# A searched order of some 2,100 steps replaced by another, v's rows regrouped by pairs of heads, and fewer small scale steps

## The chip, the cores and the metric

The kernel runs on one core of one Trainium2 chip. The metric is the device time of one execution in microseconds (us), and lower is better. The core's engines each work through a list of instructions of their own: TensorE (PE in the profile, and PEld for its weight loads), VectorE (DVE), ScalarE (ACT) and GpSimd (POOL). SyncE (SP) issues the DMA transfers, in order, from one queue.

## The reference

Pooled attention is followed by a small feed-forward layer. What is computed is:

```python
# q, k, v: 8 batches, 8 heads, 576 rows, 64 columns
k_p = k.reshape(B, H, 72, 8, D).mean(axis=3)      # v_p likewise
scores = scale * q @ k_p.T                        # 576 x 72 per head
attn = exp(scores - rowmax) / (rowsum + 1e-9)
x = (attn @ v_p).transpose(0, 2, 1, 3).reshape(4608, 512)
h = x @ w_in                                      # 512 x 1024
e = exp(h - rowmax(h)); sm = e / (sum(e) + 1e-9)
solu = h * sm
ln = (solu - mean) / sqrt(var + 1e-6) * g_ln
out = ln @ w_out                                  # 1024 x 512
```

The weights `w_in` and `w_out` arrive as 8-byte floats and are turned into pairs of 16-bit values on the chip. So are q, k, v and the tensors between the stages: each operand of a product has a high and a low half, and a product is three matmuls (high by high, high by low, low by high).

## The kernel before, in words

The 4608 rows of x are 36 tiles of 128 rows. Nine tiles cover two batches: four of the first, one that mixes the last 64 rows of both, four of the second. Each tile passes through these stages.

1. `q_hi` and `q_lo` split q, and a DMA transpose (`q_T`) turns it. For tile 0 TensorE turns it (`q_Tp`), and ScalarE copies it out (`q_Tc`).
2. `scores` (tile `sc`, 32 matmuls) writes the one score buffer in PSUM. `s_max`, `s_sub`, `s_exp`, `e_sum`, two `e_rec` and `e_mul` are the softmax on VectorE, with the exponential on ScalarE. Only after `e_mul` may the next tile's `scores` write the buffer.
3. `e_hi` (two instructions on ScalarE) and `e_lo` (two on GpSimd) split the result, and `e_T` turns it by DMA (tile 0 again by TensorE, `e_Tp` and `e_Tc`).
4. `av` (tile `xp`, 24 matmuls) multiplies by v. `x_hi` on ScalarE and `x_lo` on VectorE split the result into `xT`.
5. `mm1` (tile `hp`, 48 matmuls of 512 columns in three parts of 16) multiplies by `w_in`. The softmax-weighted activation and the statistics follow (`h_max`, `h_exp`, `z_mul` and others), and two DMA transposes turn the result.
6. `mm2` (tile `op`, 48 matmuls) multiplies by `w_out`, `o_evac` scales by the row's norm, and `o_store` writes out.

Per batch, k and v are pooled over eight rows. GpSimd does it in three levels of adds (`pool_kv`) for three pieces of each (two of 256 rows in 128 partitions, one of 64 rows). For batch 0 TensorE does it (`pool_pe`, tiles `krps` and `vrps`) and ScalarE copies it out (`pool_ev`). A power of two that bounds the pooled tensor is then found: `a_max` reduces along the row (tile `amx`), `a_par` spreads it to all partitions by a small matmul (`gk`, `gv`), `a_all` reduces again (`pk`, `pv`), and three small steps `a_scale` on VectorE make the scale and its inverse (`sk`, `sv`). `v_hi`, `v_x`, `v_lo`, `r_hi`, `r_lo`, `v_rep` and `r_put` then fill the operand `vb` of `av`.

The weights are prepared once, four pieces each. `w_exp` (`u`) and `w_sgn` run on ScalarE, `w_shift`, `w_tail` on VectorE, `w_mul` on GpSimd. `w_bnd` on TensorE finds a bound, from which `wi_scale` and `wo_scale` make the scales. `w_hi` on ScalarE writes the high half. `w_res` (tile `res`, fp32 matmuls on TensorE) and `w_lo` on ScalarE write the low half, or `w_lod` on VectorE alone for the last two pieces of `w_out`.

Nothing schedules this at run time. Each call has a number in the table `ORDER`, the calls are issued in the order of these numbers, and each engine runs its own instructions in that order. A waiting instruction therefore holds back all that stand behind it on its engine, and on SyncE all transfers behind it.

v's 576 pooled rows lie in `vr` as follows. A chunk holds two heads: 64 partitions take the first 64 pooled rows of one head, the other 64 those of the next. The last eight rows of all eight heads are a fifth chunk of 64 partitions. Each piece of two chunks is loaded by two transfers of 64 partitions.

Of the kernel before, what the change touches and what calls it, by code (L numbers as in the profile page):

```python
# [10 lines left out]
F32 = mybir.dt.float32  # L11
# [1535 lines left out]
```

## Time and profile before

| what | value |
|---|---|
| median of three runs | 493.6 us (492.75 to 493.71) |
| profiled execution, its own time | 493.96 us |
| its span, first to last instruction | 492.2 us |
| share of the span in which PE was busy | 94% |
| DVE, ACT, POOL busy | 76%, 67%, 62% |
| first `mm1` of tile 0 starts | 65.35 us |
| last matmul ends | 4.34 us before the span's end |

The span is what the trace covers. The profiled execution's own time is 1.76 us longer, and it lies 0.36 us above the median of the runs. Up to 65 us the weights are prepared, batch 0 is pooled and the pipeline is filled. From there on TensorE works through the tiles.

### The profile page before, as it was taken

The page shows a single profiled execution, that of the slowest core. Times are in us where ns is not written, and L with a number is a line of the kernel's source. Part 1 is how long each engine was busy: PE and PEld are TensorE (multiplying, and loading weights), DVE is VectorE, ACT ScalarE, POOL GpSimd, SP SyncE. Part 2 cuts the span into 40 slices and gives each one's busy share as a digit, 9 for nine tenths or more (in the row PEclk, how much of TensorE's full clock was granted, in tenths as well). Part 3 has the DMA queues.
Part 4 walks back from the last instruction along what each step waited for, and adds up shares of the span by engine and source line. Part 5 has one row for each costly group of instructions (what it writes and reads, how often), then busy time and mean ns, then how long its engine had stood idle before and what let it go on. Part 6 is the DMA issues. An engine that isn't in the chain of part 4 may idle for free.

```text
span 492.2 us, 14712 instructions
## 1 busy us (share of the span) xinstructions
PE 464.2 (94%) x5976; PEld 301.0 (61%) x5976; DVE 371.7 (76%) x808; ACT 332.2 (67%) x521; POOL 305.8 (62%) x520
## 2 busy tenths in 40 slices
PE   3698699999999999999999999999999999999996
PEld 3574355565667667766755555555566666666663
DVE  3898899997888878897859887788778769553320
ACT  4577997857867687767549656766766767674551
POOL 1556654896668686956792687554986437618340
PEclk9999899999999999999999999999999999999999
DMA  8998668997999996997979979998999485647252
GB/s 301 359 309 197 160 103 188 182 215 165 216 213 216 201 217 128 247 178 209 189 174 166 179 200 204 188 143 174 212 215 171 114 156 125 116 102 136 55 117 87
DMA packets 197940, 88.92 MB, mean 181 GB/s; under 512 B 174312, under 2 KB 182512, under 8 KB 197360
## 3 DMA queue, kind: packets, MB, share of 16 engines
q1 hardware_dynamic: 197872, 87.98, 85.8%
q8 instruction: 47, 0.77, 0.7%
q14 instruction: 21, 0.17, 0.1%
HBM read 36.70 MB, written 9.44 MB: 94 GB/s over the span
## 4 chain that ended last, share of the span: by engine, by line
PE 63%; DVE 10%; POOL 10%; DMA 7%; ACT 4%; issue 3%; SPq 2%; POOLq 0%; ACTq 0%; DVEq 0%
PE op L272 27%; PE hp L272 26%; PE xp L998 4%; PE sc L272 3%; POOL vr L395 2%; DMA wir<-in_moe_w_in_dram 2%; DMA zT<-z 2%; DMA vr<-in_v_dram 2%; POOL kr L395 2%; POOL z L1092 2%; PE vrps L405 1%; DVE z L1072 1%; DVE m L1040 1%; POOL kp L395 1%; PE res_wo L809 1%
## 5 line engine op out<-in xcount | busy, mean ns | idle before, releaser
L272 PE MATMUL hp<-wi,xT 128*64 128x512 f16 x1728 | 197.7, 379 | 1.0 <-ACT xT L1007 0.9
L272 PE MATMUL op<-wo,zT 128*64 128x512 f16 x1728 | 197.7, 379 | 0.8 <-DMA zT<-z 0.6
L272 PEld LDWEIGHTS <-xT 128*64 128x64 f16 x1728 | 110.2, 110 | 70.4 <-ACT xT L1007 1.4
L272 PEld LDWEIGHTS <-zT 128*64 128x64 f16 x1728 | 111.3, 110 | 67.0 <-DMA zT<-z 1.1
L1092 POOL TENSOR_TENSOR z<-z,z 128x512 f16<-128x512 f32 x71 | 82.8, 1175 | 56.9 <-ACT z L1086 55.5
L1040 DVE TENSOR_REDUCE m<-hp 128x1 f32<-128x1024 f32 x36 | 43.9, 1218 | 27.1 <-PE hp L272 25.1
L977 POOL TENSOR_TENSOR e<-e,e 128x512 f16<-128x512 f32 x36 | 42.6, 1184 | 31.4 <-ACT e L969 31.3
L1051 ACT ACTIVATE z<-hp,nb,Hb 128x1024 f32<-128x1024 f32 x32 | 38.3, 1198 | 20.3 <-DVE nb L1043 18.4
L1072 DVE SCALAR_TENSOR_TENSOR z<-hp,rs,z 128x1024 f32<-128x1024 f32 x36 | 46.1, 1279 | 5.9 <-ACT z L1051 4.8
L1081 ACT ACTIVATE z<-z,sz 128x1024 f32<-128x1024 f32 x36 | 41.1, 1143 | 13.3 <-DVE z L1072 13.3
L1150 ACT ACTIVATE osb<-op,f 128x512 f32<-128x512 f32 x36 | 24.5, 680 | 29.5 <-PE op L272 23.9
L395 POOL TENSOR_TENSOR kr<-kr 128x512 f32<-128x512 f32 (+3 forms) x42 | 36.9, 886 | 9.3 <-DMA kr<-in_k_dram 8.6
L395 POOL TENSOR_TENSOR vr<-vr 128x512 f32<-128x512 f32 (+3 forms) x42 | 36.7, 878 | 5.7 <-DMA vr<-in_v_dram 3.7
L1086 ACT ACTIVATE z<-z 128x1024 f16<-128x1024 f32 x36 | 37.9, 1052 | 2.0 <-issue 1.4
L933 DVE TENSOR_REDUCE sc<-sc 128x8 f32<-128x576 f32 x36 | 27.4, 761 | 14.9 <-ACT sc L929 14.9
L1105 ACT ACTIVATE junk<-z 128x1024 f16<-128x1024 f32 x36 | 37.7, 1048 | 0.2
L919 DVE TENSOR_REDUCE mx<-sc 128x8 f32<-128x576 f32 x36 | 27.0, 750 | 10.7 <-PE sc L272 10.7
L998 PEld LDWEIGHTS <-vb 128*64 128x64 f16 x960 | 29.1, 111 | 7.0 <-DMA eT<-e 1.3
L998 PE MATMUL xp<-eT,vb 128*64 128x128 f16 (+1 forms) x960 | 31.1, 215 | 1.2 <-DMA eT<-e 0.9
L272 PEld LDWEIGHTS <-qT 128*64 128x64 f16 x1152 | 25.0, 114 | 9.0 <-issue 5.1
L272 PE MATMUL sc<-kT,qT 128*64 128x72 f16 x1152 | 25.9, 200 | 3.8 <-DVE e L948 2.7
L1011 DVE SCALAR_TENSOR_TENSOR xT<-xp,xT 128x512 f16<-128x512 f32 x36 | 24.6, 683 | 5.7 <-ACT xT L1007 5.5
(239 smaller groups left out, 625.8 us busy)
## 6 DMA issues: line engine op xcount, KB each, us to landing
kr<-in_k_dram SPq DMA_DIRECT2D x16, 512.0 KB, 5.3
qr<-in_q_dram SPq DMA_DIRECT2D x16, 512.0 KB, 5.8
vr<-in_v_dram SPq DMA_DIRECT2D x32, 256.0 KB, 5.4
out_dram<-osb SPq DMA_DIRECT2D x32, 256.0 KB, 4.3
wor<-in_moe_w_out_dram SPq DMA_DIRECT2D x4, 1024.0 KB
wo<-in_moe_w_in_dram SPq DMA_DIRECT2D x2, 1024.0 KB
wir<-in_moe_w_in_dram SPq DMA_DIRECT2D x2, 1024.0 KB, 10.9
zT<-z SPq DMA_TRANSPOSE x72, 3.9
```

The lines of the kernel that those rows point to most:

```text
L272: nc.tensor.matmul(out[lo : lo + 64] if m > 64 else out, lhsT=lhsT[:, lo : lo + 64], **kw)
L395: nc.gpsimd.tensor_tensor(out=dst, in0=src[:, :, :n], in1=src[:, :, n : 2 * n], op=ALU.add)
L933: nc.vector.tensor_reduce(out=tl[i]["r0"], in_=s_view(i), axis=AX.X, op=ALU.add)
L977: nc.gpsimd.tensor_tensor(out=e_main(i, 1), in0=e_src(i)[0], in1=e_main(i, 0), op=ALU.subtract)
L998: nc.tensor.matmul(xp[64 * e : 64 * e + 64, c, lo:hi], lhsT=vb[b % 2][:, n, c, e], rhs=eT[:, 2 * c + e if n < 2 else H + c // 2, lo:hi], s ...
L1040: nc.vector.tensor_reduce(out=small(i, "m"), in_=tl[i]["hp"], axis=AX.XY, op=ALU.max)
L1051: nc.scalar.activation(z, t["hp"], AF.Exp, bias=t["nb"], scale=hsc(i, 0), accum_out=small(i, "se"))
L1072: nc.vector.scalar_tensor_tensor(out=t["z"], in0=t["hp"], scalar=t["rs"], in1=t["z"], op0=ALU.mult, op1=ALU.mult, accum_out=small(i, "sz"),)
L1081: nc.scalar.activation(t["zf"], t["zf"], AF.Identity, bias=t["sz"], scale=-float(DFF))
L1086: nc.scalar.activation(t["z16"][:, 0], t["zf"], AF.Copy)
L1092: eng.tensor_tensor(out=t["z16"][:, 1, fs], in0=t["zf"][:, fs], in1=t["z16"][:, 0, fs], op=ALU.subtract)
L1105: nc.scalar.activation(junk, t["zf"], AF.Square, scale=DFF**-0.5, accum_out=small(i, "V"))
```

## The change

Four things change.

- v: the 144 pooled rows of a pair of heads are taken as one run. Rows 8 to 135 are the pair's chunk of 128 partitions. Rows 0 to 7 and 136 to 143 go to the fifth chunk, in partitions 0 to 31 for the first head of each of the four pairs and 32 to 63 for the second. A piece of two chunks is one transfer of 128 partitions, the fifth chunk two of 32. `sel`, `e_src`, `e_rest` and the last operand of `av` follow the new places, and the second step of `e_hi` becomes two instructions.
- Small steps: `identb` carries the factor 2^-14, and `exp_bits` sets the lowest exponent itself. `a_scale` with three steps becomes `a_unit` with two. `wi_scale` and `wo_scale` lose steps, and two small products (`w_pwi`, `w_pwo`) go to GpSimd.
- `g_all` takes on the bound of `g_ln`, which stood in `wo_scale`.
- `ORDER` is new throughout. In it the three loads of batch 0's k stand otherwise among those of the weights, and v's among those of `w_out`.

```diff
 ORDER = {
-        "a_all.k": (37, 200, 454, 660, 903, 1143, 1391, 1620),
+        "a_all.k": (36, 188, 449, 652, 881, 1126, 1380, 1614),
...
-            out=dst.bitcast(I32), in0=src.bitcast(I32), scalar1=EXPMASK, scalar2=None,
-            op0=ALU.bitwise_and,
+            out=dst.bitcast(I32), in0=src.bitcast(I32), scalar1=EXPMASK, scalar2=1 << 23,
+            op0=ALU.bitwise_and, op1=ALU.bitwise_or,
...
-    nc.vector.tensor_copy(out=identb, in_=ident)
+    nc.vector.tensor_scalar(out=identb, in0=ident, scalar1=1.0 / S14, scalar2=None, op0=ALU.mult)
...
-        rows = v[b].rearrange("h (r j) d -> h r (j d)", j=POOL)
+        rows = v[b].rearrange("h (r j) d -> (h r) (j d)", j=POOL).rearrange(
+            "(c r) x -> r c x", c=CI
+        )
         if part < 2:
+            eng.dma_start(t[:, c0:c1], rows[POOL : POOL + P, c0:c1])
+        else:
             for e in range(2):
-                eng.dma_start(
-                    t[64 * e : 64 * e + 64, c0:c1],
-                    rows[2 * c0 + e : 2 * c1 : 2, :64].rearrange("c r x -> r c x"),
-                )
-        else:
-            eng.dma_start(t[:64, CI], rows[:, 64:])
+                r0 = e * (POOL + P)
+                eng.dma_start(t[32 * e : 32 * e + 32, CI], rows[r0 : r0 + POOL])
...
-    def a_scale(nm, key, n):
+    def a_unit(nm, key, n):
         st = grp[nm, key]
         if n == 0:
-            nc.vector.tensor_scalar(
-                out=st["p"], in0=st["p"], scalar1=1e-30, scalar2=1.0 / S14, op0=ALU.max,
-                op1=ALU.mult,
-            )
-        elif n == 1:
             exp_bits(st["p"], st["p"])
         else:
             nc.vector.reciprocal(out=st["s"], in_=st["p"])
...
     def wi_scale():
-        w_bound("wi")
-        nc.vector.tensor_scalar(
-            out=pwi, in0=wst["wi"]["gm"], scalar1=1.0 / S14, scalar2=None, op0=ALU.mult
-        )
+        w_bound("wi", 1.0 / S14)
         sw = const.tile([P, 1], F32, name="sw_wi")
-        nc.vector.reciprocal(out=sw, in_=pwi)
+        nc.vector.reciprocal(out=sw, in_=wst["wi"]["gm"])
         wst["wi"]["s"] = sw
-        for n, c in enumerate((2.0**-11, -(2.0**-11), 2.0**-7)):
-            nc.vector.tensor_scalar(
-                out=pw3[:, n : n + 1], in0=pwi, scalar1=c, scalar2=None, op0=ALU.mult
-            )
-
+
+    def w_pwi():
+        nc.gpsimd.tensor_scalar(
+            out=pw3, in0=c3, scalar1=wst["wi"]["gm"], scalar2=None, op0=ALU.mult
+        )
...
         else:
-            nc.scalar.activation(
-                e_rest(i)[:, ::2],
-                e_src(i)[1].unsqueeze(1).to_broadcast([P, 2, 2, HB, POOL]), AF.Copy
-            )
+            for t in (0, 2):
+                nc.scalar.activation(e_rest(i)[:, t], e_src(i)[1], AF.Copy)
...
-                            rhs=eT[:, 2 * c + e if n < 2 else H + c // 2, lo:hi],
+                            rhs=eT[:, 2 * c + e if n < 2 else H + e, lo:hi],
```

Three places of the new order follow. The first is VectorE where batch 0's v has been pooled. `amx_v`, `gv`, `pv` and `sv` are the steps of v's scale, the rows with `sc`, `mx` and `r` are the softmax of tile 1, and `q_3` and `q_2` are the low halves of q. Before:

```order
L425 TENSOR_REDUCE amx_v<-vp_89 128x1
L919 TENSOR_REDUCE mx_491<-sc_458 128x8
L487 TENSOR_REDUCE pv_502<-gv_499 128x1
L922 TENSOR_TENSOR sc_458<-sc_458,mx_491 128x2x288
L865 SCALAR_TENSOR_TENSOR q_3_507<-qr_204,sq('b', 0)_210,q_3_507 128x8x64
L686 TENSOR_REDUCE g_wo<-bnd_wo 128x1
L865 SCALAR_TENSOR_TENSOR q_2_386<-qr_204,sq('b', 0)_210,q_2_386 128x8x64
L492 TENSOR_SCALAR pv_502<-pv_502 128x1
L933 TENSOR_REDUCE sc_458<-sc_458 128x2x4
L275 TENSOR_SCALAR pv_502<-pv_502 128x1
L939 TENSOR_SCALAR sc_458<-sc_458 128x2x4
L499 RECIPROCAL sv_503<-pv_502 128x1
```

And now:

```order
L430 TENSOR_REDUCE amx_v<-vp_89 128x1
L492 TENSOR_REDUCE pv_520<-gv_517 128x1
L277 TENSOR_SCALAR pv_520<-pv_520 128x1
L499 RECIPROCAL sv_521<-pv_520 128x1
L686 TENSOR_REDUCE g_wo<-bnd_wo 128x1
```

Between the first and the last step of v's scale stood seven rows of other work and one step that the change drops. None of the eight is there now. One of the two `q` rows stands earlier, the other later.

The second place is TensorE ahead of the first `hp`, from the last fp32 product of `res_wo` that stands before `av` of tile 0. `sc` is here the scores of tile 3. Lines of three points leave out the repeats of a row. Before:

```order
L272 MATMUL sc_747<-kT_296,qT_660 64x72
...
L809 MATMUL res_wo_783<-wor_272,dg_wo_696 128x512
L812 MATMUL res_wo_783<-wo,minus 128x512
...
L998 MATMUL xp_790<-eT_723,vb_91 64x128
...
L272 MATMUL hp_819<-wi,xT_815 64x512
```

And now:

```order
L810 MATMUL res_wo_718<-wor_288,dg_wo_641 128x512
L813 MATMUL res_wo_718<-wo,minus 128x512
...
L999 MATMUL xp_727<-eT_659,vb_91 64x128
...
L274 MATMUL sc_765<-kT_300,qT_714 64x72
...
L274 MATMUL hp_803<-wi,xT_800 64x512
```

The scores of tile 3 moved from ahead of `res_wo` to between `xp` and `hp`.

The third place is the start of SyncE's queue: `wo` and `wir` are the pieces of `w_in`, `wor` those of `w_out`, `kr`, `qr` and `vr` batch 0's k, q and v. Before:

```order
L351 DMA kr_140<-in_k_dram 128x2x512
L623 DMA wo<-in_moe_w_in_dram 128x2048 x2
L355 DMA kr_140<-in_k_dram 64x512
L623 DMA wir_184<-in_moe_w_in_dram 128x2048
L351 DMA kr_140<-in_k_dram 128x2x512
L371 DMA qr_204<-in_q_dram 128x4x256 x2
L623 DMA wir_255<-in_moe_w_in_dram 128x2048
```

And now:

```order
L623 DMA wo<-in_moe_w_in_dram 128x2048 x2
L360 DMA kr_158<-in_k_dram 64x512
L623 DMA wir_169<-in_moe_w_in_dram 128x2048
L356 DMA kr_158<-in_k_dram 128x2x512 x2
L376 DMA qr_182<-in_q_dram 128x4x256 x2
L623 DMA wir_222<-in_moe_w_in_dram 128x2048
```

The first large piece of k moved from the head of the queue to behind the third piece of `w_in`, beside the second.

## Rows read from the trace of the kernel before

**Rows 1.** The page: busy time, share of the span and instructions by engine.

```profile
PE 464.2 (94%) x5976; PEld 301.0 (61%) x5976; DVE 371.7 (76%) x808; ACT 332.2 (67%) x521; POOL 305.8 (62%) x520
```

**Rows 2.** Windows: busy us of PE, PEld, DVE, ACT, POOL, then PEclk, DMA, GB/s.

```profile
40.34:65.35 25.01, 18.88 (x201) 9.01 (x200) 22.30 (x54) 20.57 (x36) 19.17 (x26) 0.93 0.69 168
65.35:487.86 422.51, 418.60 (x5554) 269.65 (x5554) 320.63 (x690) 285.91 (x456) 272.14 (x478) 1.00 0.87 171
487.86:492.20 4.34, 0.00 (x0) 0.00 (x0) 0.00 (x0) 0.69 (x1) 0.00 (x0) 0.92 0.17 62
```

**Rows 3.** Timeline of PE: start, duration, what, idle before and its releaser.

```profile
15.13 3.79 PE L405 MATMUL krps<-kr,ident 128*128 128x128 f32 x16 [1.14 <-DMA kr<-in_k_dram]
...
37.73 0.44 PE L272 MATMUL g_g<-ident,g_g 128*64 128x128 f32 x4
38.10 0.37 PE L650 MATMUL bnd_wo<-pmat,u_wo 128*128 128x32 bf16 x8
38.31 2.03 PE L405 MATMUL vrps<-vr,ident 128*128 128x128 f32 x16
...
41.50 0.25 PE L272 MATMUL gv<-identb,amx_v 128*64 128x128 bf16 x2 [0.52 <-DVE amx_v L425]
...
45.55 0.44 PE L272 MATMUL g_wo<-ident,g_wo 128*64 128x128 f32 x4 [0.98 <-DVE g_wo L686]
...
49.99 0.38 PE L812 MATMUL res_wi<-wi,minus 128*128 128x512 f16 x1 [0.68 <-ACT wi L788]
...
52.49 0.71 PE L272 MATMUL sc<-kT,qT 128*64 128x72 f16 x32 [1.01 <-DVE e L948]
53.94 1.46 PE L809 MATMUL res_wo<-wor,dg_wo 128*128 128x512 f32 x2 [0.73 <-POOL vr L395]
...
60.73 0.71 PE L272 MATMUL sc<-kT,qT 128*64 128x72 f16 x32 [1.53 <-DVE e L948]
...
65.35 3.64 PE L272 MATMUL hp<-wi,xT 128*64 128x512 f16 x32 [0.69 <-ACT xT L1007]
```

**Rows 4.** Timeline of PE near the end.

```profile
466.94 20.91 PE L272 MATMUL op<-wo,zT 128*64 128x512 f16 x192
```

**Rows 5.** Timeline of DVE from the pooling of batch 0's v.

```profile
40.95 0.49 DVE L425 TENSOR_REDUCE amx_v<-vp 128x1 bf16<-128x320 f32 x1 [2.28 <-ACT vp L416]
...
42.88 2.28 DVE L865 SCALAR_TENSOR_TENSOR q<-qr,sq('b', 0)_210,q 128x512 f16<-128x512 f32 x1
...
45.42 1.81 DVE L865 SCALAR_TENSOR_TENSOR q<-qr,sq('b', 0)_210,q 128x512 f16<-128x512 f32 x1
...
48.09 0.15 DVE L499 RECIPROCAL sv<-pv 128x1 f32<-128x1 f32 x1
```

**Rows 6.** Timelines of POOL and ACT in the same stretch.

```profile
42.10 2.51 POOL L395 TENSOR_TENSOR kr<-kr 64x256 f32<-64x256 f32 x3
45.41 1.28 POOL L395 TENSOR_TENSOR vr<-vr 128x512 f32<-128x512 f32 x1 [0.80 <-DMA vr<-in_v_dram]
...
48.34 0.51 ACT L568 ACTIVATE vb<-vp,sv 64x256 f16<-64x256 f32 x1 [2.67 <-DVE sv L499]
```

**Rows 7.** Groups on DVE and ACT by line: busy, mean ns of one.

```profile
L865 DVE SCALAR_TENSOR_TENSOR q<-qr,sq('b', 7)_7329,q 128x512 f16<-128x512 f32 x4 | 2.9, 736 | 1.7 <-ACT q L861 1.7
L492 DVE TENSOR_SCALAR pv<-pv 128x1 f32<-128x1 f32 x8 | 1.2, 150 | 0.1
L971 ACT ACTIVATE e<-e 128x128 f16<-128x128 f32 x36 | 10.8, 299 | 7.4 <-DVE e L948 5.4 <-POOL f L1126 1.0 <-DMA eT<-e 1.0
```

**Rows 8.** Windows: TensorE's clock between 54 and 58 us; DVE up to 120 us.

```profile
54.00:56.00 2.00, 2.00 (x4) 0.97 (x5) 1.93 (x6) 1.47 (x4) 1.12 (x2) 0.64 1.05 218
56.00:58.00 2.00, 2.00 (x5) 0.26 (x3) 1.36 (x4) 1.50 (x3) 1.26 (x1) 0.50 0.76 220
65.35:120.00 54.65, 52.98 (x764) 32.59 (x766) 51.38 (x112) 42.74 (x68) 37.85 (x62) 1.00 0.95 181
```

**Rows 9.** The tile vr: issue of v's transfers, ns min/median/max.

```profile
L360 SPq DMA_DIRECT2D vr<-in_v_dram x32: 596/615/2004, 13.2 to 355.7; - x32
```

More of the change, by code (lines that the diff above doesn't have):

```diff
@@ new lines @@
+        1852, 1920, 1939, 1997, 1972),
+        "e_T": (221, 239, 275, 332, 402, 425, 572, 497, 628, 712, 641, 761, 825, 873, 933, 957,
+        1078, 1145, 1146, 1248, 1263, 1356, 1406, 1476, 1495, 1557, 1647, 1634, 1718, 1748, 1851,
+        1887, 1908, 1996, 1942),
+        "e_Tc": (181,),
+        "e_Tp": (180,),
+        "e_hi": (107, 108, 218, 219, 237, 222, 273, 272, 329, 330, 399, 373, 423, 422, 509, 508,
[4 rows of a table added]
+        "e_lo": (109, 220, 238, 274, 331, 401, 424, 571, 496, 604, 711, 640, 760, 824, 861, 932,
@@ new lines @@
+        926, 1023, 1106, 1049, 1200, 1238, 1274, 1345, 1425, 1379, 1502, 1581, 1564, 1655, 1704,
+        1784, 1824, 1864, 1954, 1917),
+        "g_T": (93,),
+        "g_all": (122,),
+        "g_max": (96,),
+        "g_par": (121,),
+        "g_put": (94,),
+        "h_bat": (245, 283, 679, 904, 1060, 1182, 1535, 1839),
+        "h_exp": (265, 325, 362, 441, 457, 545, 614, 623, 697, 751, 857, 828, 936, 954, 1005,
+        1037, 1151, 1185, 1258, 1300, 1384, 1402, 1486, 1510, 1612, 1618, 1679, 1796, 1720, 1832,
@@ new lines @@
+        1823),
+        "v_rep": (192, 318, 542, 833, 1101, 1243, 1498, 1847),
+        "v_x": (214, 196, 296, 328, 586, 607, 879, 849, 1166, 1172, 1286, 1247, 1625, 1540, 1828,
+        1821),
+        "w_all.wi": (66,),
+        "w_all.wo": (143,),
+        "w_bnd.wi": (47, 48, 49, 52),
+        "w_bnd.wo": (73, 126, 127, 136),
+        "w_dg.wi": (68,),
+        "w_dg.wo": (175, 145),
+        "w_exp.wi": (1, 8, 13, 41),
+        "w_exp.wo": (55, 78, 88, 104),
+        "w_hi.wi": (117, 90, 74, 106),
@@ new lines @@
+        "w_hi.wo": (151, 149, 240, 310),
+        "w_lo.wi": (150, 132, 89, 172),
+        "w_lo.wo": (249, 174),
+        "w_load": (0, 6, 12, 40, 54, 77, 86, 103),
+        "w_lod.wo": (344, 324, 321, 316),
+        "w_mul.wi": (5, 19, 17, 64),
+        "w_mul.wo": (61, 84, 156, 251),
+        "w_par.wi": (65,),
+        "w_par.wo": (138,),
+        "w_pwi": (69,),
+        "w_pwo": (353,),
+        "w_res.wi": (148, 125, 75, 171),
+        "w_res.wo": (210, 173),
+        "w_rmax.wi": (53,),
@@ new lines @@
+        "w_rmax.wo": (137,),
+        "w_sgn.wi": (2, 7, 15, 63),
+        "w_sgn.wo": (60, 83, 111, 246),
+        "w_shift.wi": (3, 9, 14, 42),
+        "w_shift.wo": (56, 81, 98, 105),
+        "w_tail.wi": (4, 18, 16, 51),
+        "w_tail.wo": (58, 82, 110, 250),
+        "wi_scale": (67,),
+        "wo_scale": (144,),
+        "x_hi": (226, 258, 277, 334, 384, 464, 507, 589, 563, 662, 782, 723, 843, 895, 953, 981,
+        1013, 1112, 1191, 1207, 1288, 1330, 1399, 1434, 1513, 1547, 1629, 1702, 1658, 1757, 1788,
@@ L325 @@
     nc.gpsimd.memset(phalf, -0.5)
+    for n, c in enumerate((2.0**-11, -(2.0**-11), 2.0**-7)):
+        nc.gpsimd.memset(c3[:, n : n + 1], c)
     for t in vp:
@@ L1211, in scale @@
                 w=[("p" + nm, key), ("s" + nm, key)])
-        for j in range(3):
-            n_ = op("dve", 0.16, t + 0.7 + 0.2 * j, a_scale, nm, key, j, u=[("p" + nm, key)],
+        for j in range(2):
+            n_ = op("dve", 0.16, t + 0.7 + 0.2 * j, a_unit, nm, key, j, u=[("p" + nm, key)],
                     w=[("s" + nm, key)], after=[n_])
@@ L1319, in weight @@
         if nm == "wi":
-            op("dve", 0.9, t_sum + 0.8, wi_scale, r=[("g2", nm)], w=[("ws", nm)])
+            op("dve", 0.5, t_sum + 0.8, wi_scale, r=[("g2", nm)], w=[("ws", nm)])
+            op("pool", 0.3, t_sum + 1.5, w_pwi, r=[("ws", nm)], w=[("pw3",)])
         else:
@@ L1326, in weight @@
             op("dve", 0.28, t_sum - 2, g_all, r=[("x", "gg")], w=[("gg2",)])
-            op("dve", 1.2, t_sum + 0.8, wo_scale, r=[("g2", nm), ("gg2",)], w=[("ws", nm)])
+            op("dve", 0.5, t_sum + 0.8, wo_scale, r=[("g2", nm), ("gg2",)], w=[("ws", nm)])
+            op("pool", 0.3, t_sum + 1.5, w_pwo, r=[("ws", nm)], w=[("pwo",)])
         if nm == "wi" and any((nm, c) not in LO_DVE for c in range(4)):
```

311 lines of the change are left out of this document (134 added, 177 removed), and 90 rows, old and new, of the table ORDER.

## The prediction

> **What bounds the kernel now.** I read the page first. TensorE is busy 94% of the span, and no other engine is above 76% [rows 1]. So TensorE is the first suspect, and what counts is where it stood idle. The windows answer that [rows 2]. I cut the span at three points: the end of the last pooling product of batch 0's v (38.31 + 2.03 = 40.34 us), the first `mm1` (65.35 us) and the end of the last `mm2` [rows 3, 4]. From 65.35 us on TensorE is busy 418.60 of 422.51 us, so 3.91 us are idle there. Behind the last matmul come 4.34 us of evacuation and store. In the 25.01 us before the first `mm1` TensorE is busy 18.88 and idle 6.13. The end of the kernel is therefore the start of the first `mm1`, plus a fixed amount of matmul work, plus 3.91 us of idle time, plus 4.34.
>
> The 6.13 us are told one by one by the timeline of PE [rows 3]: 0.52 (`gv` waits for `amx_v`), 0.98 (`g_wo`), 0.68 (`res_wi` waits for ScalarE's `w_hi`), 1.01 and 1.53 (`scores` of tiles 2 and 3 wait until `e_mul` has freed the score buffer), 0.73 (`res_wo`) and 0.69 (`mm1` waits for `x_hi`). They sum to 6.14.
>
> Behind these waits stands VectorE. `amx_v` runs at 40.95, but v's inverse scale is ready only after 48.09 + 0.15 [rows 5]. Two low halves of q stand in between, and they take 2.28 and 1.81 us [rows 5] where the undisturbed form takes 0.74 [rows 7]. During both GpSimd pools k and v [rows 6]. They lose 1.54 + 1.07 = 2.6 us. ScalarE waits 2.67 us for that scale, with `w_hi` behind [rows 6].
>
> **What stays the same.** The count of matmuls of every kind is unchanged. In both orders three `scores`, three `res_wi`, two `res_wo`, one `av` and the small products lie between the last pooling product and the first `mm1`, and the last four tiles of `mm2` close the program as one block of 192 matmuls [rows 4]. I cost the tail at 0.
>
> **Term A, the start of the first `mm1`.** I go through the idle times with the new order.
>
> - `scores` of tile 3 stands behind `av` now. Its 0.71 us of work cover the wait for `x_hi`, and it no longer waits for `e_mul`: 1.53 + 0.69 = 2.2 us less.
> - `gv` stands behind one `res_wi` (two pairs of rows, over 2 us of work) instead of next to `scores`: 0.5 less.
> - The `w_hi` that was late behind ScalarE's wait for v's scale stands ahead of that wait: 0.7 less.
> - `g_wo`, `scores` of tile 2 and `res_wo` keep their 0.98 + 1.01 + 0.73, since the steps that they wait for are still the last ready.
> - One group of bound products and `g_g` move from ahead of 40.34 to behind it: 0.37 + 0.44 = 0.8 more [rows 3].
> - The first `res_wi` now stands ahead of all v pooling and waits for `wi_scale`, while k's pooling starts later. A large piece of k takes TensorE 3.79 us early in the program [rows 3], and both large pieces now arrive back to back. The bounds are 0 (transfers hide it) and 3.8 (one whole piece late). The total of bytes ahead of the last piece of `w_in` is unchanged, and one of the two pieces can start before the other lands, so I take 0.8, near the lower end.
> - The granted clock is 0.64 and 0.50 from 54 to 58 us, after a stretch of idle waits [rows 8]. [...] With fewer waits ahead this may not happen. Bounds: 0 and 1.7 less. I take 0.8 less.
>
> Sum: -2.2 - 0.5 - 0.7 + 0.8 + 0.8 - 0.8 = -2.6 us. The first `mm1` starts at about 62.7.
>
> **Term B, idle time behind it.** It can fall by 3.9 at most. It can grow, because VectorE is busy 51.38 of 54.65 us up to 120 us [rows 8]: a pipeline that starts 2.6 us earlier needs 2.6 us less VectorE time. There are two sources. Up to the eighth `h_max`, eleven small steps fewer stand in VectorE's list (three each of k's and v's scales, four of `wi_scale`, two of `wo_scale`, and one product more). At 0.15 each [rows 7] that is 1.65 us. The two stalls of the low halves are another 2.6, if they don't come back. 4.25 is more than 2.6, so the idle time should not grow. I take a quarter off: -1.0. Bounds: -3.9 and +2.6.
>
> **Costed at nothing.** The second step of `e_hi` is two instructions for one of 0.30 [rows 7], at most 0.3 us more per tile on ScalarE. ScalarE has 136.6 us idle of 422.51 [rows 2], so this hides behind the matmuls of tiles ahead. Without that cover it would be 36 x 0.3 = 10.8 us. The large pieces of v need one issue for two of 0.62 [rows 9], and the small one two for one, so SyncE issues four transfers per batch instead of five, while TensorE works on earlier tiles. One product per weight on GpSimd (`w_pwi`, `w_pwo`) is first needed by `h_bat` and `n_f`, behind `mm1`.
>
> **Sum.** The profiled execution took 493.96, 1.76 of it outside the span. 493.96 - 2.6 - 1.0 = 490.4. The median of the runs lay 0.4 below the profiled one, so I predict 490.0. The measurement can tell about 0.2% (1 us) from no change, so "faster" is below 492.6.
>
> **Rivals.**
>
> *More.* The order takes nearly all waits away: A = -5.3 (the kept 2.7 go too), and B = -2.6, two thirds of the idle time. That gives 493.6 - 7.9 = 485.7. For it: none of the waits is a transfer from memory. Against: VectorE's 94% busy stretch. Chance 0.17.
>
> *Given back.* The start is earlier by 2.6, but VectorE is no further at 120 us, because its relief doesn't come true, and B grows by 2.6: 493.6. For it speaks the same 94%. Chance 0.13.
>
> *Stalls move.* The order only shifts the collisions: GpSimd keeps its adds, and other steps of VectorE last longer instead. Then VectorE's relief is the small steps alone, and A keeps only the move of `scores` with the extra work, -2.2 + 0.8 = -1.4: 492.2. The low half of q shows what a collision costs: it ended 0.55 us after the three adds of 2.51 us that began at 42.10 [rows 5, 6], so it waited for more than one of them. [...] Chance 0.10.
>
> *Slower.* k is late. If the second large piece of k starts only when the first is through, and both at the slow rate of 3.79, then k's scale, its transpose, the four bounds of `w_in` behind them on TensorE, `wi_scale` and the first `res_wi` all move by 3.8, and the waits behind keep their length because ScalarE's list (weights, exponentials, v) is late with them. The one saving that is left is that of `scores`, against 0.8 of moved work: 493.6 + 3.8 + 0.8 - 2.2 = 496.0. It decides where the last pooling product of v ends more than 2.6 us after 40.34. For it: both pieces behind the third piece of `w_in`. Against: the first has its data earlier. Chance 0.13.
>
> **How the numbers follow.** The forecast has 0.47, with a range of its own of 488.0 to 492.2. With "more" (0.17) and "stalls move" (0.10) it makes most of "faster": 0.72. "Same" is most of "given back" and the upper edge of "stalls move": 0.13. "Slower" is k's delay and the rest: 0.15. The range reaches from "more" to just past "given back": 485.5 to 494.5. It leaves out k's delay and a little below.
>
> **What would show it.** In the changed kernel the first `mm1` starts between 61 and 64 us. No low half of q beside v's scale lasts over 1 us, and `sv` comes within 2 us of `amx_v`. No idle stands ahead of the `scores` of tile 3 or the first `mm1`. The idle time from there to the last `mm2` is 2 to 4 us, and the tail is 4.3 us. I am wrong if the first `mm1` starts later than 65, or if TensorE idles more than 5 us behind it.

## The result and the profile after

The changed kernel took 487.04 us (median of 4 runs, 485.28 to 487.35), the kernel before 493.65 beside it. The ratio is 0.9872, with a 95% interval of 0.9842 to 0.9902. A repetition of six runs gave 486.76 against 491.88, ratio 0.9894 (0.9873 to 0.9914). The forecast was 490.0, 3.6 us less than before. Measured were 6.6 and 5.1 less. The sign and the range held. The size of the gain and the place where part of it came from did not. Times, medians and ratios here and below are of executions in the chip's faster state; one of e10_old_order_v's twelve (498.44 us) was in the slower one and is left out.

The page of the kernel after, busy time by engine as in [rows 1]:

```profile
PE 456.5 (94%) x5976; PEld 287.7 (59%) x5976; DVE 372.2 (77%) x787; ACT 335.2 (69%) x557; POOL 304.5 (63%) x525
```

VectorE has 21 instructions fewer, 787 for 808, and not less busy time. The windows of after, cut at the end of v's last pooling product, the first `mm1` and the last `mm2`, with the columns of [rows 2]:

```profile
0.00:37.57 37.57, 20.65 (x214) 17.30 (x216) 29.58 (x60) 26.60 (x34) 16.12 (x22) 0.95 0.99 351
37.57:58.15 20.58, 17.55 (x214) 9.15 (x214) 18.30 (x43) 17.29 (x33) 17.15 (x21) 1.00 0.70 152
58.15:120.00 61.85, 58.77 (x842) 35.49 (x844) 60.19 (x126) 46.59 (x81) 40.60 (x70) 1.00 0.91 167
120.00:479.62 359.62, 359.57 (x4716) 225.74 (x4712) 264.08 (x560) 244.05 (x411) 230.59 (x415) 1.00 0.86 172
479.62:483.60 3.98, 0.00 (x0) 0.00 (x0) 0.00 (x0) 0.69 (x1) 0.00 (x0) 1.00 0.18 66
```

Against [rows 2] three things moved. v's pooling ends 2.77 us earlier (37.57 for 40.34). The stretch from there to the first `mm1` is 4.43 us shorter: 3.10 of that is idle time (20.58 - 17.55 = 3.03, it was 6.13), and 1.33 is busy time. Behind the first `mm1` 3.08 + 0.05 = 3.13 us are idle, where 3.91 were. The tail is 3.98 for 4.34.

The timeline of PE in after, which answers to [rows 3, 4] (start, duration, what, idle before and its releaser):

```profile
32.46 5.11 PE L410 MATMUL vrps<-vr,ident 128*128 128x128 f32 x48
...
42.55 0.44 PE L274 MATMUL g_wo<-ident,g_wo 128*64 128x128 f32 x4 [0.80 <-DVE g_wo L686]
45.81 0.71 PE L274 MATMUL sc<-kT,qT 128*64 128x72 f16 x32 [0.40 <-DVE e L949]
...
52.08 0.72 PE L883 MATMUL eTp<-ident,e 128*128 128x128 f16 x10 [0.90 <-ACT wi L824]
53.44 0.44 PE L274 MATMUL vr<-vr,sel 128*64 128x64 f16 x16 [0.47 <-DVE pk L492]
56.59 0.86 PE L999 MATMUL xp<-eT,vb 128*64 128x128 f16 x24 [0.28 <-ACT e L975]
57.29 0.69 PE L274 MATMUL sc<-kT,qT 128*64 128x72 f16 x32
58.15 1.92 PE L274 MATMUL hp<-wi,xT 128*64 128x512 f16 x16 [0.17 <-ACT xT L1008]
60.55 1.92 PE L274 MATMUL hp<-wi,xT 128*64 128x512 f16 x16 [0.49 <-DVE xT L1012]
...
458.73 20.89 PE L274 MATMUL op<-wo,zT 128*64 128x512 f16 x192
```

The waits of `gv`, `res_wi`, `res_wo` and of the last `scores` are gone. Small new ones stand at `eTp`, `vr` and `xp`, and inside the first `mm1` (0.49). VectorE, GpSimd and ScalarE in after, which answer to [rows 5, 6]:

```profile
40.16 0.48 DVE L430 TENSOR_REDUCE amx_v<-vp 128x1 bf16<-128x320 f32 x1
42.01 0.16 DVE L499 RECIPROCAL sv<-pv 128x1 f32<-128x1 f32 x1
...
46.61 2.17 DVE L866 SCALAR_TENSOR_TENSOR q<-qr,sq('b', 0)_206,q 128x512 f16<-128x512 f32 x1
...
56.57 1.53 DVE L866 SCALAR_TENSOR_TENSOR q<-qm,sq('m', 0)_665,q 128x512 f16<-128x512 f32 x1
...
45.80 1.19 POOL L400 TENSOR_TENSOR kp<-kr 128x128 f32<-128x128 f32 x3
46.95 2.43 POOL L400 TENSOR_TENSOR vr<-vr 128x512 f32<-128x512 f32 x2
...
56.33 1.22 POOL L978 TENSOR_TENSOR e<-e,e 128x512 f16<-128x512 f32 x1 [3.04 <-ACT e L972]
...
50.37 0.72 ACT L930 ACTIVATE sc<-sc,ct('b', 0)_317 128x576 f32<-128x576 f32 x1 [1.38 <-DVE sc L923]
```

v's scale is ready 2.0 us after `amx_v` began, where it took 7.3. The long low halves of q did not vanish. Two last 2.17 and 1.53 us, the first beside GpSimd's pooling, the second beside an `e_lo`. TensorE now waits behind each of them. The first holds back the maximum and the subtraction of tile 2's softmax on VectorE. ScalarE waits 1.38 us for that (the row at 50.37), evacuates `wi` only then, and `eTp` waits 0.90 us for this. The second holds back `x_lo`, for which the second part of `mm1` waits 0.49 us. The trace shows these chains; no run moved the two low halves to price them.

Of the signs that the prediction named, three held: v's scale came in time, no low half beside it was long, and no idle stood ahead of the `scores` of tile 3. The first `mm1` came earlier than the 61 to 64 us (58.15, and 59.76 in the repetition), with 0.17 us of idle ahead of it. The idle time behind it was 3.13 and 4.23 us where 2 to 4 were named, and the tail 3.98 where 4.3 was.

### The profile page after: what moved, and what is told of

The parts are those of the page before. It is cut to its first block, busy times and chain, and to the rows that moved or that the text cites. A ratio compares the mean times of both kernels' runs of the same rounds, so it can differ in the third digit from the quotient of the medians.

```text
span 483.6 us, 14740 instructions
## 1 busy us (share of the span) xinstructions
PE 456.5 (94%) x5976; PEld 287.7 (59%) x5976; DVE 372.2 (77%) x787; ACT 335.2 (69%) x557; POOL 304.5 (63%) x525
## 4 chain that ended last, share of the span: by engine, by line
PE 78%; DVE 16%; DMA 2%; issue 2%; ACT 1%; SPq 0%; POOL 0%; ACTq 0%; DVEq 0%
PE op L274 35%; PE hp L274 31%; PE xp L999 4%; PE sc L274 3%; DMA kr<-in_k_dram 2%; DVE q L866 2%; DVE m L1041 1%; PE krps L410 1%; DVE sc L934 1%; DVE mx L920 1%; DVE sc L923 1%; DVE z L1073 1%; DVE e L949 1%; PE vrps L410 1%; PE res_wi L810 1%
## 5 line engine op out<-in xcount | busy, mean ns | idle before, releaser
L274 PEld LDWEIGHTS <-xT 128*64 128x64 f16 x1728 | 106.6, 110 | 75.2 <-ACT xT L1008 2.0
L274 PEld LDWEIGHTS <-zT 128*64 128x64 f16 x1728 | 106.5, 110 | 70.6 <-DMA zT<-z 0.5
L1008 ACT ACTIVATE xT<-xp 128x512 f16<-128x512 f32 x36 | 21.2, 589 | 12.2 <-PE xp L999 12.2
```

What stands on the lines that cost most here:

```text
L274: nc.tensor.matmul(out[lo : lo + 64] if m > 64 else out, lhsT=lhsT[:, lo : lo + 64], **kw)
```

## The experiments

Twelve kernels ran. Where a kernel has another table, it is printed more densely, so its line numbers are smaller by 102 for the same code. The runs were taken in three groups with a `before` of their own, so times of different groups are compared by the ratio. The table gives the medians, the ratio to before in the same runs, and three places of each profile: the end of v's last pooling product, the first `mm1`, and the idle time of TensorE from there to the last `mm2`.

| run | us | before | ratio (95%) | v pooled | first mm1 | idle behind |
|---|---|---|---|---|---|---|
| e9_after_again | 486.76 | 491.88 | 0.9894 (0.9873 to 0.9914) | 39.16 | 59.76 | 4.23 |
| e1_old_order | 489.99 | 492.34 | 0.9953 (0.9928 to 0.9978) | 40.33 | 64.44 | 2.26 |
| e2_new_order | 490.94 | 492.34 | 0.9967 (0.9946 to 0.9988) | 40.98 | 64.19 | 3.62 |
| e3_k_first | 488.09 | 492.34 | 0.9917 (0.9888 to 0.9945) | 40.88 | 61.48 | 3.24 |
| e4_v_wo_loads | 487.66 | 492.34 | 0.9908 (0.9882 to 0.9935) | 39.78 | 62.64 | 2.76 |
| e5_v_halves | 493.02 | 493.39 | 0.9996 (0.9967 to 1.0026) | 42.45 | 61.96 | 6.36 |
| e6_v_chunks | 488.00 | 493.39 | 0.9889 (0.9850 to 0.9928) | 38.53 | 59.14 | 4.74 |
| e7_old_steps | 488.21 | 493.39 | 0.9896 (0.9858 to 0.9934) | 38.37 | 60.80 | 3.04 |
| e8_scores3 | 487.79 | 493.39 | 0.9885 (0.9850 to 0.9921) | 38.62 | 60.53 | 2.64 |
| e10_old_order_v | 491.65 | 491.88 | 0.9993 (0.9962 to 1.0024) | 38.83 | 62.84 | 2.86 |
| e11_qlo | 489.78 | 491.88 | 0.9965 (0.9950 to 0.9980) | 38.83 | 63.77 | 3.05 |
| e12_v_early | 486.58 | 491.88 | 0.9895 (0.9872 to 0.9918) | 33.07 | 59.26 | 3.25 |

### Order or code: e1_old_order and e2_new_order

My first theory was that the order makes nearly all of the gain. The first run takes the code of after with the numbers of before, the second the code of before with the numbers of after.

```diff
 e1_old_order, against after
-        "a_unit.k": (39, 57, 211, 213, 451, 455, 657, 663, 882, 890, 1129, 1155, 1390, 1437, 1615,
+        "a_unit.k": (51, 56, 209, 215, 457, 460, 662, 682, 905, 906, 1193, 1194, 1393, 1403, 1665,
...
-        "w_pwi": (69,),
-        "w_pwo": (353,),
+        "w_pwi": (68.5,),
+        "w_pwo": (149.5,),
...
 e2_new_order, against before
-        "a_scale.k": (43, 51, 56, 207, 209, 215, 456, 457, 460, 661, 662, 682, 904, 905, 906,
+        "a_scale.k": (39, 39.2, 57, 211, 211.2, 213, 451, 451.2, 455, 657, 657.2, 663, 882, 882.2,
...
```

All other numbers are those of the other kernel.

> The changed code (v in pairs of heads, fewer small steps) in the order of before. Theory: the order makes nearly all of the 6.6 us, because in the trace of after the waits that went (scores of tile 3, gv, w_hi, the clock dip) are waits behind other instructions. Then this run gives 492.5 to 493.9, and the first mm1 stays at 64.5 to 65.5 us. Rival: the code makes it, by eleven small steps fewer ahead of the eighth h_max and by fewer v transfers. Then it gives 488 to 491, with v's last pooling product near 38 us instead of 40.3.

> The code of before (v in single heads by two transfers per piece, three small scale steps) in the order of after; the third scale step stands next to the other two. Theory (order): 487 to 488.5, with the first mm1 at 58 to 59.5 us. Rival (code): 490 to 493, since v's extra issue of 0.62 us and each extra small step lie on the path to the first mm1.

Both theories fell, and both rivals held by their times, though v's last product did not come near 38 us in the first (40.33). The code alone gives 2.3 us, the order alone 1.4 to 1.6, and both together 5.1 to 6.6. Either half seems to be worth more with the other; against the repetition alone the difference lies within the intervals. The trace of the second run shows one reason. Windows from 26 to 30 us, first of e2_new_order, then of after; the last column is GB/s, the one ahead of it the busy share of the DMA engines:

```profile
26.00:28.00 2.00, 0.00 (x0) 0.00 (x0) 1.86 (x11) 2.00 (x4) 1.52 (x1) 0.50 1.08 233
28.00:30.00 2.00, 1.52 (x41) 1.48 (x42) 0.65 (x2) 2.00 (x3) 2.00 (x2) 0.50 1.11 215
```

```profile
26.00:28.00 2.00, 0.33 (x12) 0.36 (x14) 1.42 (x6) 2.00 (x4) 1.96 (x1) 0.79 1.02 386
28.00:30.00 2.00, 2.00 (x37) 1.40 (x33) 1.09 (x2) 2.00 (x3) 2.00 (x2) 0.50 1.05 409
```

The DMA share is 1.02 to 1.11 in both, yet 233 and 215 GB/s are moved where v comes by two transfers of 64 partitions, for 386 and 409 in after. The kernel before has the same dip, from 22 to 26 us:

```profile
22.00:24.00 2.00, 1.23 (x16) 0.86 (x12) 2.00 (x4) 2.00 (x3) 0.34 (x1) 1.00 1.07 208
24.00:26.00 2.00, 1.73 (x22) 1.69 (x24) 2.00 (x4) 2.00 (x3) 0.00 (x0) 1.00 1.11 226
```

In the new order v's last piece is late by it, as the timeline of PE in e2_new_order shows:

```profile
37.77 3.21 PE L303 MATMUL vrps<-vr,ident 128*128 128x128 f32 x16 [1.29 <-DMA vr<-in_v_dram]
```

### The sequence of the loads: e3_k_first and e4_v_wo_loads

```diff
 e3_k_first
-        "load_kv": (21, 20, 10, 112, 100, 99, 152, 157, 154, 197, 201, 205, 294, 295, 293, 342,
+        "load_kv": (-1, 20, 10, 112, 100, 99, 152, 157, 154, 197, 201, 205, 294, 295, 293, 342,
...
 e4_v_wo_loads
-        "load_kv": (21, 20, 10, 112, 100, 99, 152, 157, 154, 197, 201, 205, 294, 295, 293, 342,
+        "load_kv": (21, 20, 10, 75.7, 100, 75.6, 152, 157, 154, 197, 201, 205, 294, 295, 293, 342,
...
-        "w_load": (0, 6, 12, 40, 54, 77, 86, 103),
+        "w_load": (0, 6, 12, 40, 54, 77, 86, 87.5),
```

> After with one number changed: the first large piece of k is loaded ahead of all weights, as in before. The forecast charged the new place of k with 0.8 us, but v's last pooling product came 2.8 us earlier. Theory: the place of k is neutral, since the bytes ahead of v are the same: 486 to 488, last vrps within 0.7 us of 37.6. Rival: the back-to-back arrival of k is itself what brought the start forward: 489 or more, last vrps at 39.5 to 40.5.

> After with v's and w_out's loads in the sequence of before (two pieces of v behind w_out's first, then w_out's other three, then v's last large piece). Theory: this sequence is what made the last large piece of v late: in before its issue stood behind w_out's last piece at 24.03 us (22.50 in after), and moved bytes fell to 208 and 226 GB/s. Then the last vrps ends at 39 to 40.5 and the time is 488.5 to 490. Rival: the sequence of loads is hidden, and the start is early because of what TensorE does first: 486.5 to 487.8, last vrps still near 37.6.

The first `mm1` came 1.7 and 2.9 us later than in the repetition of after, and TensorE had 1.0 and 1.5 us less idle time behind it. By the ratios the times lie 1.1 and 0.7 us above after's, with intervals that overlap. So both sequences are a small part of the time. At the start they show more. In the first run v's last product ended at 40.88, even later than the rival had it, and the time lies between the two branches. In the second it ended at 39.78, as the theory had it, behind a wait for v's data, but the time is the rival's. The timeline of PE in e4_v_wo_loads:

```profile
34.67 5.11 PE L308 MATMUL vrps<-vr,ident 128*128 128x128 f32 x48 [1.34 <-DMA vr<-in_v_dram]
```

### How v is transferred: e5_v_halves and e6_v_chunks

Two transfers per piece in both, of 256 KB each. In the first each fills 64 partitions, in the second 128.

```diff
 e5_v_halves
-            eng.dma_start(t[:, c0:c1], rows[POOL : POOL + P, c0:c1])
+            for e in range(2):
+                eng.dma_start(
+                    t[64 * e : 64 * e + 64, c0:c1],
+                    rows[POOL + 64 * e : POOL + 64 * e + 64, c0:c1],
+                )
 e6_v_chunks
-            eng.dma_start(t[:, c0:c1], rows[POOL : POOL + P, c0:c1])
+            for c in range(c0, c1):
+                eng.dma_start(t[:, c], rows[POOL : POOL + P, c])
```

> After, with each large piece of v loaded by two transfers of 64 partitions (lower and upper half) in place of one of 128; where the data go is unchanged. The run with the old code in the new order showed 215 to 241 GB/s from 26 to 32 us, where after kept 386 to 412, and v's last product 3.4 us later. Theory (64-partition transfers move at half the rate): the low stretch comes back, v's last pooling product ends at 40 to 41.5 us, the first mm1 starts at 61 to 64.5, and the time is 489.5 to 491.5. Rival (the layout or the small steps made the difference): 486.5 to 488, no low stretch.

> After, with each large piece of v loaded by two transfers of 128 partitions and one chunk each: as many issues and as many bytes per transfer as in the run with halves, but all 128 partitions in each. Theory (partitions decide): about 400 GB/s through, as after, 486.5 to 488. Rival (the number of issues on SyncE or the size of a transfer decides): as the run with halves, 489 or more.

This pair decides it. With halves the whole gain is gone (0.9996), with chunks nothing is lost (0.9889). That is 1.07% or 5.3 us for the number of partitions in a transfer, at an equal number of issues and bytes. It is more than the theory had (489.5 to 491.5, with v's last product by 41.5; it ended at 42.45). Not all of it lies in front: the first `mm1` is 2.8 us later with halves, and 1.6 us more are idle behind it. A second pair prices the transfers lower: e2_new_order and e7_old_steps below have the same order and the same small steps, and differ in v's rows and transfers, by 0.71% or 3.5 us. A window of e5_v_halves, the last product of v there (timeline of PE), and the same window and v's products in e6_v_chunks:

```profile
28.00:30.00 2.00, 1.77 (x41) 1.73 (x42) 0.65 (x2) 2.00 (x3) 2.00 (x2) 0.50 1.03 199
```

```profile
38.94 3.51 PE L414 MATMUL vrps<-vr,ident 128*128 128x128 f32 x16 [2.46 <-DMA vr<-in_v_dram]
```

```profile
28.00:30.00 2.00, 1.80 (x41) 1.75 (x42) 0.64 (x2) 2.00 (x3) 2.00 (x2) 0.50 1.03 406
```

```profile
33.42 5.11 PE L411 MATMUL vrps<-vr,ident 128*128 128x128 f32 x48
```

199 GB/s against 406, at a DMA share of 1.03 in both. With halves the product waits 2.46 us for v and then takes 3.51 at a clock of 0.50 to 0.66, where the same 16 matmuls took 2.03 in before [rows 3], at 1.00. In the windows shown, 199 to 233 GB/s go with transfers of 64 partitions and 386 to 409 with those of 128. Why the first move fewer bytes, no run shows.

### The small steps and the scores of tile 3: e7_old_steps and e8_scores3

```diff
 e7_old_steps
         if n == 0:
+            nc.vector.tensor_scalar(
+                out=st["p"], in0=st["p"], scalar1=1e-30, scalar2=1.0 / S14, op0=ALU.max,
+                op1=ALU.mult,
+            )
             exp_bits(st["p"], st["p"])
...
 e8_scores3
-        "scores": (72, 119, 167, 224, 287, 337, 388, 473, 429, 522, 647, 565, 692, 767, 802, 837,
+        "scores": (72, 119, 167, 209.5, 287, 337, 388, 473, 429, 522, 647, 565, 692, 767, 802, 837,
...
-        "s_max": (79, 120, 168, 225, 288, 348, 389, 474, 430, 523, 648, 566, 693, 768, 803, 839,
+        "s_max": (79, 120, 168, 209.6, 288, 348, 389, 474, 430, 523, 648, 566, 693, 768, 803, 839,
...
```

In the first, `wi_scale`, `wo_scale`, `exp_bits` and `identb` are also as before, and `w_pwi` and `w_pwo` issue nothing.

> After, with the small steps of before (three steps per scale of k and v, the three products of w_in's scale and the product of w_out's on VectorE), v as in after. Theory (v's transfers make the code's share): the steps are worth 0 to 1.5 us, 487 to 488.5, first mm1 at 58 to 60. Rival (the steps relieve VectorE in its 94% stretch, as the forecast had it with 1.65 us and more): 489 to 491, with the idle time behind the first mm1 at 4.5 us or more.

> After, with the scores of tile 3 and its maximum ahead of the last residual of w_out and of av, as in before. The forecast priced this move at 2.2 us (1.53 of waiting for e_mul and 0.69 for x_hi). In after e_mul of tile 2 ends at 54.67, so scores in that place would wait some 0.9 us, and mm1 behind av another 0.6. Theory: 1.2 to 2.2 us slower than after, 488.2 to 489.5. Rival: the wait only moves on (the last residual and e_T give it back), 486.5 to 487.8.

The base of these two and of the runs below is after, repeated:

> After, unchanged, as the base of the three runs beside it. Its profiled execution at first (485.28) lay 1.8 below its median; runs with the same order and full transfers of v had v's last product end at 38.4 to 38.6 us, not 37.57. Expected: 486.5 to 488, last vrps at 37.5 to 38.7, first mm1 at 58 to 59.5.

Neither changes the time by an amount that can be measured (0.9896 and 0.9885 beside 0.9894); by the intervals about 2 us either way would go unseen. Both do change the start. Windows from v's last product to the first `mm1` and from there to 120 us, of e9_after_again, e7_old_steps and e8_scores3:

```profile
39.16:59.76 20.60, 17.55 (x214) 9.15 (x214) 18.33 (x43) 17.27 (x33) 17.18 (x21) 1.00 0.71 148
59.76:120.00 60.24, 56.06 (x818) 33.84 (x820) 57.18 (x123) 44.82 (x78) 40.36 (x68) 1.00 0.95 169
```

```profile
38.37:60.80 22.43, 17.55 (x213) 9.15 (x214) 20.02 (x46) 17.23 (x33) 18.00 (x23) 1.00 0.56 133
60.80:120.00 59.20, 56.22 (x818) 33.95 (x820) 57.46 (x125) 44.00 (x77) 39.15 (x64) 1.00 0.90 172
```

```profile
38.62:60.53 21.91, 17.75 (x214) 9.18 (x214) 19.08 (x44) 17.24 (x33) 17.46 (x23) 1.00 0.58 137
60.53:120.00 59.47, 57.28 (x828) 34.59 (x830) 57.84 (x123) 44.93 (x78) 39.45 (x65) 1.00 0.93 174
```

The small steps cost 1.8 us in the first stretch and the scores 1.3. In the second stretch TensorE is idle 2.98 and 2.19 us, where after has 4.18. So 1.2 and 2.0 us are given back. VectorE is busy 95 to 97% there in all three, which speaks for it as what sets the pace, and in after 2.3 us of TensorE's waits there end with a step of VectorE. That was not tried by itself.

The repetition also shows how far a single profile reaches: its first `mm1` starts at 59.76, that of the first profile at 58.15, with the same 20.6 us ahead of it. That and the end of v's products (39.16) lie just past what I expected. The first profiled execution was the shortest of its four.

### v's transfers alone: e10_old_order_v

The code is that of e7_old_steps, the numbers are those of e1_old_order (the first of the three steps stands with the second):

```diff
-        "av": (215, 257, 276, 333, 383, 463, 506, 573, 561, 661, 775, 702, 842, 893, 952, 977,
+        "av": (234, 269, 277, 341, 368, 481, 512, 598, 583, 666, 755, 716, 856, 923, 942, 953,
...
```

> The order and the small steps of before, with v's rows and transfers of after: one part of the change alone. Theory: a faster transfer is worth nothing where the product that reads it stands behind other work, and in the order of before v's last large product does (38.30 us in both before and the run with the new code in the old order). Then 491.5 to 493.5, and the 2.3 us of that run are the small steps'. Rival: the faster transfers gain by themselves, at the start or in the seven later batches: 489.5 to 491.

0.9993: alone the faster transfers bring nothing that can be measured. In the old order the last large product of v stands behind `res_wi`, the bounds and `g_g`, and reads a piece that has landed in either case. (In its profile that product ended at 38.83, not at 40.3 as I expected; its median lies 1.3 us above that profile.) The 2.3 us of e1_old_order would then be the small steps', but the two intervals overlap, so that stays open.

### The low halves of q: e11_qlo

```diff
-        "q_hi": (37, 43, 59, 133, 191, 260, 248, 335, 355, 447, 515, 487, 550, 690, 758, 787, 813,
+        "q_hi": (37, 43, 59, 125.5, 191, 260, 248, 335, 355, 447, 515, 487, 550, 690, 758, 787, 813,
...
-        "q_lo": (38, 44, 85, 165, 216, 270, 298, 351, 356, 460, 540, 521, 554, 699, 762, 789, 814,
+        "q_lo": (38, 44, 130.4, 131.5, 216, 270, 298, 351, 356, 460, 540, 521, 554, 699, 762, 789, 814,
...
```

> After, with the low halves of q of tiles 2 and 3 put back between the steps of v's scale, where GpSimd multiplies a piece of w_out and adds k (40.57 to 45.8 us in after). Theory (collisions at the port): one or both last 1.5 to 2.3 us instead of 0.75, v's scale is ready 2 to 4 us later, the first mm1 starts 1 to 3 us later, and the time is 488 to 490.5. Rival: the delay is given back behind the first mm1, where VectorE sets the pace in any case: 486.5 to 488, as the run with scores moved back showed.

That the two engines meet at a port, no run shows; what the trace has is that a step of VectorE and adds of GpSimd lasted longer side by side (2.75 us for 0.74, 3.92 for 3.18). In its times the theory held: 0.9965 against 0.9894, with intervals apart, 3.0 us slower by the medians and 3.5 by the ratios. The first `mm1` came 4.0 us later, more than the 1 to 3 expected. VectorE, GpSimd and PE of e11_qlo, then two windows:

```profile
42.96 2.75 DVE L764 SCALAR_TENSOR_TENSOR q<-qr,sq('b', 0)_206,q 128x512 f16<-128x512 f32 x1
45.69 1.14 DVE L764 SCALAR_TENSOR_TENSOR q<-qr,sq('b', 0)_206,q 128x512 f16<-128x512 f32 x1
46.76 0.15 DVE L397 RECIPROCAL sv<-pv 128x1 f32<-128x1 f32 x1
...
41.81 2.13 POOL L576 TENSOR_TENSOR wor<-wor,sg_wo 128x1024 f32<-128x1024 f32 x1
43.90 3.92 POOL L298 TENSOR_TENSOR kr<-kr 128x512 f32<-128x512 f32 x4
...
47.29 0.70 PE L172 MATMUL g_wo<-ident,g_wo 128*64 128x128 f32 x4 [4.28 <-DVE g_wo L584]
```

```profile
38.83:63.77 24.94, 19.83 (x212) 9.92 (x212) 19.50 (x44) 17.72 (x33) 17.14 (x20) 0.86 0.46 120
...
48.00:50.00 2.00, 2.00 (x3) 0.77 (x4) 1.79 (x9) 0.95 (x3) 0.93 (x3) 0.50 0.76 225
```

The first low half began 1.15 us into GpSimd's multiply and ended 1.8 us behind its end, while the four adds that follow were running. The four took 3.92 us, and 3.18 in after. `g_wo` stands behind on VectorE, and TensorE waits 4.28 us for it, 0.80 in after. After that wait the granted clock is at 0.50, and the busy time of the stretch grows from 17.55 to 19.83. So collisions of 2.4 us (2.75 + 1.14 - 2 x 0.74), with the two low halves' own 1.5 us now ahead of `g_wo`, made the stretch 4.3 us longer: 2.06 by idle time, 2.28 by busy time at the lower clock. Behind the first `mm1` 1.2 came back.

### An attempt at a better order: e12_v_early

```diff
-        "load_kv": (21, 20, 10, 112, 100, 99, 152, 157, 154, 197, 201, 205, 294, 295, 293, 342,
+        "load_kv": (21, 20, 10, 54.3, 54.2, 54.1, 152, 157, 154, 197, 201, 205, 294, 295, 293, 342,
...
-        "pool_pe": (25, 23, 11, 113, 101, 102),
+        "pool_pe": (25, 23, 11, 113, 71.2, 71.1),
```

> After, with v loaded right behind w_out's first piece, ahead of its other three, and two of the three v products ahead of the first scores, where TensorE waits 3.19 us for kT (24.48 to 27.67 us in after). Theory: v has landed by 23 to 24 us, these 3.2 us of products fill the wait, and the first mm1 comes 1.5 to 3 us earlier; 484.5 to 486.5. Rival: ScalarE has no idle time from 19 to 43 us in after (only 0.33 us ahead of one exponential) and is the next bound, or VectorE behind mm1 gives it back: 486.5 to 488.

No gain (0.9895). Two of v's products did fill the wait ahead of the first scores. The timeline of PE in e12_v_early:

```profile
24.25 3.12 PE L308 MATMUL vrps<-vr,ident 64*64 64x64 f32 x32
27.44 0.71 PE L172 MATMUL sc<-kT,qT 128*64 128x72 f16 x32
31.02 2.05 PE L308 MATMUL vrps<-vr,ident 128*128 128x128 f32 x16
35.80 0.71 PE L172 MATMUL sc<-kT,qT 128*64 128x72 f16 x32 [2.73 <-DMA qT<-q]
...
46.91 0.71 PE L172 MATMUL sc<-kT,qT 128*64 128x72 f16 x32 [1.58 <-DVE e L847]
```

v was pooled by 33.07, but the next scores wait 2.73 us for q's DMA transpose, which I had left out of account. The first `mm1` came 0.5 us earlier, not 1.5 to 3. Neither ScalarE nor VectorE, which my rival named, ended that wait.

## Why the prediction was right, and where it was not

The mechanism was right: waits of TensorE ahead of the first `mm1` go with the new order, 3.1 us of them where 3.4 were forecast. Some of the sizes were not.

**The term that failed: the start, +0.8.** The stretch behind v's last product was to start 0.8 us later (bounds 0 to 3.8). It started 2.8 us earlier, and 1.2 in the repetition. Three things the forecast had wrong or left out there.

First, a slip of the sum. The bound products and `g_g` were charged with 0.8 us behind 40.34 and never taken off ahead of it. The first `mm1` stands behind both places, so their move costs it nothing. Without the slip the same sum gives A = -3.4 and 489.2 us.

Second, k's new place was taken for a delay. The first `scores` need k's pooled rows. The timelines of PE of before, after, e9_after_again and e3_k_first, where k's first piece is back at the head of the queue:

```profile
28.74 1.17 PE L272 MATMUL sc<-kT,qT 128*64 128x72 f16 x32 [0.28 <-ACT qT L891]
27.67 1.17 PE L274 MATMUL sc<-kT,qT 128*64 128x72 f16 x32 [3.19 <-DVE kT L536]
28.81 1.17 PE L274 MATMUL sc<-kT,qT 128*64 128x72 f16 x32 [3.25 <-DVE kT L536]
30.54 1.17 PE L172 MATMUL sc<-kT,qT 128*64 128x72 f16 x32 [3.28 <-DVE kT L434]
```

Against before they start 1.1 us earlier and 0.1 later. Within the new order the old place costs 1.7 us, one profile each.

Third, v's loads were costed at nothing. I counted their issues on SyncE (0.62 us, hidden) and not the time that the bytes take. The forecast took for granted that v's data are there for products that the new order puts earlier. In after they are, so this did not spoil the number. But it is the condition for it: with transfers of 64 partitions TensorE waits 1.29 us (e2_new_order) and 2.46 (e5_v_halves) for them, and the latter has no gain left. The dip to 208 and 226 GB/s stood in the trace of before. I had read the DMA engines' busy share (1.07 and 1.11 there), which shows nothing of it. What else made the start earlier was not taken apart.

**Term A, from v's last product to the first `mm1`.** Forecast -2.2 - 0.5 - 0.7 + 0.8 - 0.8 = -3.4, measured -4.4. Idle time fell by 3.1, as forecast (3.4), though not wait by wait: of the kept 2.7 (`g_wo`, `scores` of tile 2, `res_wo`) 1.2 is left, and `eTp`, `vr` and `xp` wait for 1.65 instead. The clock term was mis-sized. This stretch ran at 1.00 throughout (0.93 before [rows 2, 8]), and busy time fell by 1.33 in spite of 0.8 of moved work. That is 2.1, past the bound of 1.7 (0.36 x 2 + 0.50 x 2 at the clocks of [rows 8]), where 0.8 was taken, an estimate between that and nothing.

**The move of `scores`.** Its two waits went as forecast (0 and 0.17 left), its worth is not shown. 1.3 us of the start hang on it, and nothing of the time that can be measured.

**VectorE's relief.** The small steps bring the first `mm1` forward and nothing measurable in the end. The stalls of the low halves, the other source, are worth 3.0 to 3.5 us of time. In the sum they stood only in the waits of term A and in a share of B, and the clock behind them (0.50 in e11_qlo) was not counted with them.

**Term B.** -1.0 forecast, -0.8 measured in the first profile, +0.3 in the repetition. The latter has a wait of 1.4 us for the DMA transpose of `zT` that the first profile has not.

**The rivals.** "More" had A at -5.3 and B at -2.6. A was -7.2 and -5.6, B stayed small, and the time lies between it and the forecast. "Given back" is what e7_old_steps and e8_scores3 show in part. "Stalls move" was right in that other low halves last 2.17 and 1.53 us now, with 0.90 and 0.49 us of TensorE's idle time behind them, and wrong on the price, since the other waits went all the same; in e11_qlo a low half again lasted into the GpSimd adds behind the multiply that it met. The chance of 0.10 was the author's estimate; why a step of one engine lasts longer beside the other, no run shows. "Slower" did not come: v's last product ended before 40.34.

That 490.0 came out only 3 us off is in part luck, since errors of opposite sign met: 2.2 us for a move of `scores` whose worth no run could measure, against a start set 2.0 to 3.6 us too late and a clock term 1.3 us too small. What is shown: the transfers are worth 5.3 us in the new order by one pair of runs and 3.5 by another, and nothing measurable in the old one; the order without them 1.4 to 1.6; the place of the low halves 3.0 to 3.5 within the new order. These are no parts of one sum, since each was taken with the others in place. What sets the pace behind the first `mm1`, and what the small steps are worth in the old order, stays open.

## What to carry to other kernels

Read GB/s beside the DMA share: loading v with 64 partitions per transfer in place of 128 left the share at 1.03 and moved 199 GB/s for 406 (e5_v_halves and e6_v_chunks, 28 to 30 us). Price a change of transfers and a change of order together, since here the faster transfers paid (5.3 us by e5_v_halves and e6_v_chunks, nothing measurable in e10_old_order_v) only where the instruction that reads them was next, and the earlier instruction only where its data were there. Charge work that moves across a cut of the timeline on one side and take it off on the other. A wait taken away while the pipeline fills may be given back where a busier engine follows (1.2 and 2.0 us in e7_old_steps and e8_scores3), and one left ahead of TensorE can cost its clock as well: 0.50 behind the 4.28 us of e11_qlo.

## What was not expected of the hardware

- Where v came by two transfers of 64 partitions, 199 to 233 GB/s were moved in the windows shown, with two of 128 partitions and the same bytes 406, at a DMA share of 1.03 to 1.11 in all of them.
- A two-input step of VectorE ended 1.8 us behind the end of the GpSimd multiply that it met in e11_qlo, while the adds behind that were running (2.75 us for 0.74). GpSimd was slower as well: four adds took 3.92 us there, and 3.18 in after.
- In e11_qlo 4.28 us without a matmul were followed by a granted clock of 0.50 up to 52 us, which cost 2.28 us of busy time.
